# The first two token tiles loaded as rows and turned on TensorE, with the early loads on two queues paced by the warm-up matmuls

## The chip, the cores and the metric

The kernel runs on one core of a Trainium2 chip. The metric is the device time of one execution in microseconds. Where the mean granted clock of an execution was below 0.999 the text says so. "Same" means within 2% by a 95% interval. Times inside an execution count from the start of the core's span.

## The reference, cut to what matters

Two attentions over the same tokens, mixed by a gate. S is 2048 tokens, D is 1024, there are 32 heads of 32, all in bf16.

```
g = sigmoid((x * gate_w).sum(-1, keepdims=True))
a = A(x, A_wqkv, A_wo)     # linear attention, feature map elu + 1
b = B(x, B_wqkv, B_wo)     # each token attends to 8 tokens, 2 apart, backwards
out = g * a + (1 - g) * b
```

Both attentions begin with x @ wqkv. The kernel starts with the v columns of B: x (2048x1024) times 1024 columns of B_wqkv. Only the first 15 us of this product matter here.

## The kernel before

The kernel's matmuls contract over the partitions, so a tile of 128 tokens is needed turned: 128 features on the partitions, 128 tokens along the row, eight such blocks for 1024 features. The kernel lets the DMA do this (a transposing load for each of 16 token tiles, all on SyncE's queue). The weights of the first stage come in two halves of 512 columns. Each half comes in four pieces of 256 KB; a piece holds two of the eight contraction blocks.

The kernel is written as a list of operations with modelled costs and priorities; a small scheduler in the kernel's own source decides the order on every engine before the program is built. `P.op(engine, function, cost, reads, writes, prio, ...)` adds one operation.

```python
def load_x(t, prio):                        # one tile of 128 tokens, turned by the DMA
    e_, r = t // 8, t % 8
    return P.op("sp", lambda e: e.dma_start_transpose(xT[:, :, t * 128:(t + 1) * 128], x2[e_, r * 128:(r + 1) * 128, :]), 1.5, ...)

def load_w(slot, half, src, c0, prio, d0=0, d1=8, eng="sp", after=()):   # blocks d0..d1 of one half
    return P.op(eng, lambda e: e.dma_start(ws[slot][:, d0:d1, half * 512:half * 512 + 512], src[:, d0:d1, c0:c0 + 512]), ...)

load_x(0, 0)
load_w(0, 0, Bw, 2048, 0.1, 0, 2, "act")    # piece 1
load_w(0, 0, Bw, 2048, 0.2, 2, 4, "act")    # piece 2
load_w(0, 0, Bw, 2048, 0.3, 4, 6)           # piece 3
load_w(0, 0, Bw, 2048, 0.4, 6, 8)           # piece 4
for t in range(1, NT):
    load_x(t, 3 + t)
for d in range(0, 8, 2):                    # the second half, four pieces
    load_w(0, 1, Bw, 2560, 6.1 + 0.1 * d, d, d + 2)
...
for i in range(WARM):                       # WARM = 11, on a zeroed tile
    P.op("pe", lambda e: e.matmul(banks[7].ap(), warm[:, 0:128], warm[:, :], start=True, stop=True), 0.43, ...)
...
for t, half in [(4 * b + i, half) for b in range(NT // 4) for half in range(2) for i in range(4)]:
    ...
    step = 2 if t == 0 else 8               # tile 0 goes by pieces, the others in groups of 8
    for d in range(0, 8, step):
        o = group(bank, xs, w, [xr, ws[0].part((d, d + step), (half * 512, half * 512 + 512))], d, d + step)
```

So TensorE's order is: tiles 0 to 3 with the first half (32 matmuls of 128x512), tiles 0 to 3 with the second half (32 more), then tiles 4 to 7, and so on. The program fixes this order for TensorE.

## Time and profile before

| | before |
|---|---|
| median of 6 executions | 486.65 us (486.50 to 487.02) |
| TensorE busy in the profiled execution | 474.2 of 485.2 us |
| share of TensorE in the chain that ended last | 95% |
| first real matmul starts | 5.54 us |
| matmuls without a gap from | 15.30 us |

The page of the kernel before gives the busy time of each engine with its share of the span and its instruction count, and the shares of the chain that ended last:

```profile
span 485.2 us, 10105 instructions
PE 474.2 (98%) x4339; PEld 222.8 (46%) x4403; DVE 285.2 (59%) x547; ACT 140.2 (29%) x227; POOL 5.9 (1%) x36
...
PE 95%; SPq 2%; issue 1%; DMA 1%; ACT 0%; DVE 0%
```

TensorE (PE) is the bound, and its work is fixed. What is left to win is the time in which it has nothing to multiply, and that lies at the front. The timeline of TensorE shows it. Columns: start, length, engine, line, operation, out and in, shapes, number of instructions, and in brackets the idle time before with what ended it. L1373 is the warm-up, L1334 the real product.

```profile
1.25 4.01 PE L1373 MATMUL ps_all<-warm 128*128 128x512 bf16 x11 [1.25 <-DVE warm L1283]
5.54 1.47 PE L1334 MATMUL ps_all<-w,xT 128*128 128x512 bf16 x6 [0.28 <-DMA xT<-in_A_x_dram]
7.25 0.60 PE L1334 MATMUL ps_all<-w,xT 128*128 128x512 bf16 x2 [0.24 <-DMA w<-in_B_wqkv_dram]
8.17 6.82 PE L1334 MATMUL ps_all<-w,xT 128*128 128x512 bf16 x30 [0.32 <-DMA xT<-in_A_x_dram]
15.30 9.01 PE L1334 MATMUL ps_all<-w,xT 128*128 128x512 bf16 x41 [0.30 <-DMA w<-in_B_wqkv_dram]
```

Tile 0 waits for its transposing load until 5.54, then for the last weight piece until 7.25; tile 1 waits for its own load until 8.17; and the second weight half stops TensorE twice more, at 14.39 (inside the fourth line; 0.17 us over the pace) and just before 15.30. One record just before 15.30 is missing from the trace; by the spacing of the starts, 15.30 is the 40th real matmul.

A useful single number follows: matmuls of 512 columns start every 0.2158 us, so the 40th would start at 15.30 if the first had started at 15.30 - 39 x 0.2158 = 6.88 us and nothing had waited. I call this the clean start. Before: 6.88.

The issue of loads on SyncE's queue, from its timeline of the kernel before (columns as above; a DMA_TRANSPOSE is a tile of x, the others are weight pieces):

```profile
0.80 1.38 SPq L1308 DMA_TRANSPOSE xT<-in_A_x_dram  x1
2.24 1.06 SPq L1313 DMA_DIRECT2D w<-in_B_wqkv_dram  x2
3.35 4.92 SPq L1308 DMA_TRANSPOSE xT<-in_A_x_dram  x3
8.31 2.12 SPq L1313 DMA_DIRECT2D w<-in_B_wqkv_dram  x4
```

A transposing load holds the queue 1.25 to 2.27 us, a plain one about 0.5 us. The end of the windowed chain of waits of the kernel before (start, length, what) says which of these the 40th matmul hung on:

```profile
4.64 2.27 SPq L1308
...
8.31 0.58 SPq L1313
...
9.96 5.07 DMA w<-in_B_wqkv_dram
...
15.30 4.91 PE ps_all L1334 x22
```

### The profile page before, as it was taken

The page shows a single profiled execution, that of the slowest core. Times are in us where ns is not written, and L with a number is a line of the kernel's source. Part 1 is how long each engine was busy: PE and PEld are TensorE (multiplying, and loading weights), DVE is VectorE, ACT ScalarE, POOL GpSimd, SP SyncE. Part 2 cuts the span into 40 slices and gives each one's busy share as a digit, 9 for nine tenths or more (in the row PEclk, how much of TensorE's full clock was granted, in tenths as well). Part 3 has the DMA queues.
Part 4 walks back from the last instruction along what each step waited for, and adds up shares of the span by engine and source line. Part 5 has one row for each costly group of instructions (what it writes and reads, how often), then busy time and mean ns, then how long its engine had stood idle before and what let it go on. Part 6 is the DMA issues. An engine that isn't in the chain of part 4 may idle for free.

```text
span 485.2 us, 10105 instructions
## 1 busy us (share of the span) xinstructions
PE 474.2 (98%) x4339; PEld 222.8 (46%) x4403; DVE 285.2 (59%) x547; ACT 140.2 (29%) x227; POOL 5.9 (1%) x36
## 2 busy tenths in 40 slices
PE   8999999999999999999999999999999999999997
PEld 3444444444444444454544554444444444444443
DVE  2121435888688888665666556496579236653434
ACT  2111121235322234334443333455532230111000
POOL 4000000000000000000000000000000000000000
PEclk9999999999999999999999999999999999999999
DMA  8999993132014459433222322820086018830212
GB/s 224 222 194 299 309 355 122 65 110 86 1 44 135 107 138 245 100 76 86 55 75 67 85 66 66 204 54 2 10 217 163 1 15 242 221 24 2 88 68 89
DMA packets 72951, 57.39 MB, mean 118 GB/s; under 512 B 37953, under 2 KB 60865, under 8 KB 72898
## 3 DMA queue, kind: packets, MB, share of 16 engines
q1 hardware_dynamic: 72210, 56.07, 44.3%
q8 instruction: 36, 0.59, 0.5%
q10 hardware_dynamic: 688, 0.59, 0.4%
q14 instruction: 17, 0.14, 0.1%
HBM read 34.49 MB, written 13.76 MB: 99 GB/s over the span
## 4 chain that ended last, share of the span: by engine, by line
PE 95%; SPq 2%; issue 1%; DMA 1%; ACT 0%; DVE 0%
PE ps_all L1334 78%; PE ps_all L1693 11%; PE ps_all L1463 2%; PE ps_all L1440 2%; SPq L1308 1%; DMA w<-in_B_wqkv_dram 1%; PE ps_all L1556 1%; SPq L1313 1%; PE ps_all L1638 0%; PE ps_all L1610 0%; ACT e L1341 0%; DVE o L1697 0%
## 5 line engine op out<-in xcount | busy, mean ns | idle before, releaser
L1334 PE MATMUL ps_all<-w,xT 128*128 128x512 bf16 x924 | 208.6, 379 | 4.5 <-issue 2.1
L1334 PE MATMUL ps_all<-xT,w 128*128 128x512 bf16 x745 | 166.3, 379 | 2.2 <-issue 1.4
L1334 PEld LDWEIGHTS ps_all<-w,xT 128*128 128x128 bf16 x960 | 91.2, 98 | 111.1 <-DMA w<-in_B_wqkv_dram 2.1
L1334 PEld LDWEIGHTS ps_all<-xT,w 128*128 128x128 bf16 x768 | 73.9, 98 | 88.7 <-issue 1.3
L1693 PE MATMUL ps_all<-w,qT 128*128 128x512 bf16 (+1 forms) x260 | 55.4, 372 | 0.2
L1693 PEld LDWEIGHTS ps_all<-w,qT 128*128 128x128 bf16 x264 | 25.9, 98 | 29.6
L1365 DVE CAST vst<-ps_all 128x512 bf16<-128x512 f32 x15 | 10.4, 694 | 43.5 <-PE ps_all L1334 43.5
L1448 ACT ACTIVATE E<-ps_all 128x1824 bf16<-128x1824 f32 (+1 forms) x18 | 30.4, 1689 | 13.4 <-PE ps_all L1440 13.4
L1345 DVE TENSOR_SCALAR e<-e 128x512 bf16<-128x512 bf16 x64 | 18.4, 290 | 26.9 <-ACT e L1343 14.0
L1697 DVE SCALAR_TENSOR_TENSOR o<-ps_all,gm,xT 128x512 bf16<-128x512 f32 (+1 forms) x25 | 18.0, 728 | 21.1 <-PE ps_all L1693 20.8
L1341 ACT ACTIVATE e<-ps_all 128x512 bf16<-128x512 f32 x32 | 19.1, 598 | 39.0 <-PE ps_all L1334 38.1
L1343 ACT ACTIVATE e<-ps_all 128x512 bf16<-128x512 f32 x32 | 19.1, 598 | 32.3 <-PE ps_all L1334 32.3
L1295 DVE TENSOR_TENSOR mx<-mx,kT 128x1024 bf16<-128x1024 bf16 x32 | 20.9, 688 | 10.9 <-ACT kT L1366 10.8
L1295 DVE TENSOR_TENSOR mx<-mx,qT 128x1024 bf16<-128x1024 bf16 x32 | 20.8, 687 | 7.9 <-ACT qT L1369 7.9
L1451 DVE TENSOR_TENSOR E<-E,msk 128x1824 bf16<-128x1824 bf16 (+1 forms) x18 | 19.9, 1104 | 7.8 <-ACT E L1448 7.4
L1366 ACT ACTIVATE vst<-ps_all 128x512 bf16<-128x512 f32 x17 | 10.2, 601 | 48.5 <-PE ps_all L1334 45.1
L1480 DVE TENSOR_TENSOR ot<-ps_all,rs 128x512 bf16<-128x512 f32 x36 | 23.3, 686 | 0.0
L1366 ACT ACTIVATE az<-ps_all 128x512 bf16<-128x512 f32 x22 | 13.2, 601 | 34.5 <-PE ps_all L1334 34.5
L1366 ACT ACTIVATE kT<-ps_all 128x512 bf16<-128x512 f32 x20 | 11.9, 597 | 37.6 <-PE ps_all L1334 37.6
L1347 DVE SCALAR_TENSOR_TENSOR pk<-ps_all,e 128x512 bf16<-128x512 f32 x32 | 22.0, 689 | 0.7
L1369 ACT ACTIVATE qT<-ps_all 128x512 bf16<-128x512 f32 x19 | 11.4, 598 | 37.4 <-PE ps_all L1334 37.3
L1369 ACT ACTIVATE xT<-ps_all,g 128x512 bf16<-128x512 f32 x10 | 6.9, 689 | 45.1 <-PE ps_all L1334 45.1
(72 smaller groups left out, 260.2 us busy)
## 6 DMA issues: line engine op xcount, KB each, us to landing
rb<-rc_hbm SPq DMA_DIRECT2D x32, 256.0 KB, 5.2
w<-in_A_wqkv_dram SPq DMA_DIRECT2D x6, 1024.0 KB, 9.0
v<-vB_hbm SPq DMA_DIRECT2D x36, 132.0 KB, 2.7
vB_hbm<-vst SPq DMA_DIRECT2D x32, 132.0 KB, 6.2
w<-in_B_wqkv_dram SPq DMA_DIRECT2D x4, 1024.0 KB, 9.5
xn<-in_A_x_dram SPq DMA_DIRECT2D x16, 256.0 KB, 2.7
out_dram<-o SPq DMA_DIRECT2D x15, 256.0 KB, 2.1
oB_hbm<-ot SPq DMA_DIRECT2D x36, 96.0 KB, 2.2
```

The lines of the kernel that those rows point to most:

```text
L1295: P.op("dve", lambda e, m=m, op=op: e.tensor_tensor(m[:, 0:n], m[:, 0:n], src, op), 0.08 + n / 1920.0, reads=[m.all(), reg], writes=[m.all()],
L1334: last = e.matmul(bank.ap(), lhs(dc), rhs(dc), start=(dc == 0), stop=(dc == 7))
L1341: P.op("act", lambda e: e.activation(e_[:, :], bank.ap(), ACT.Exp), act(512), reads=[bank.iv], writes=[e_.all()])
L1343: P.op("act", lambda e: e.activation(e_[:, :], bank.ap(), ACT.Exp, accum_out=qe[:, col:col + 1]), act(512) + 0.1, reads=[bank.iv], writes= ...
L1345: P.op("dve", lambda e: e.tensor_scalar(e_[:, :], e_[:, :], 1.0, 1e-6, op0=ALU.min, op1=ALU.add), 0.25, reads=[e_.all()], writes=[e_.all()])
L1347: P.op("dve", lambda e: e.scalar_tensor_tensor(out=dst, in0=bank.ap(), scalar=0.0, in1=e_[:, :], op0=ALU.max, op1=ALU.add), dps(512), read ...
L1366: fa = lambda e: e.activation(dst, src(), ACT.Copy)
L1369: fa = lambda e: e.activation(dst, src(), ACT.Copy, scale=scale)
L1448: P.op("act", lambda e: e.activation(E[:, 0:32 * nq].rearrange("p (j q) -> p j q", j=4), ps[:, 4:8, 0:8 * nq], ACT.Exp), act(32 * nq), rea ...
L1451: P.op("dve", lambda e: e.tensor_tensor(ev(), ev(), m[:, :, :].rearrange("p r q -> p (r q)")[:, None, :].to_broadcast([128, 16, 2 * nq]), ...
L1480: P.op("dve", lambda e, r=r, bv=bv, h=h: e.tensor_tensor(o[:, 512 * h:512 * h + 512].rearrange("p (k i c) -> p k i c", k=2, c=32), bv()[:, ...
L1693: last = e.matmul(bank.ap(0, f1 - f0), qT[:, dc, t * 128:(t + 1) * 128], ws[3][:, dc, f0:f1], start=(dc == 0), stop=(dc == 7))
```

## The change

The intent: tiles 0 and 1 need not be turned by the slow transposing load. They are loaded plain, as rows, and TensorE turns them by multiplying with an identity (`out = rows.T @ ident`); VectorE and ScalarE copy the result out of PSUM. SyncE's queue is then free earlier for tiles 2 and 3 and for the second weight half. The first six loads are shared between SyncE's and ScalarE's queues, and the last four of them wait for a warm-up matmul each. The warm-up shrinks from 11 to 6 matmuls, since the turns go on from there. The makers of the window masks leave GpSimd's start. The core of the diff:

```diff
-    WARM = 11
+    WARM = 6
...
+        C("pool", lambda e: e.memset(ident[:, :], 0.0), 0.1, [ident.all()])
+        C("pool", lambda e: e.affine_select(out=ident[:, :], ..., compare_op=ALU.not_equal, fill=1.0, ...), 0.3, ...)
...   (the makers of the window masks move behind tile 8)
-        load_x(0, 0)
-        load_w(0, 0, Bw, 2048, 0.1, 0, 2, "act")
-        load_w(0, 0, Bw, 2048, 0.2, 2, 4, "act")
-        load_w(0, 0, Bw, 2048, 0.3, 4, 6)
-        load_w(0, 0, Bw, 2048, 0.4, 6, 8)
-        for t in range(1, NT):
-            load_x(t, 3 + t)
+        warms = [P.op("pe", <warm-up matmul>, 0.43, ...) for _ in range(WARM)]
+        def pace(o, i):
+            if i >= 0:
+                o.deps.add(warms[i])
+            ...
+        due(load_rows(0, 0, 1024, 0, "act"), 0.45, 2.7)
+        due(pace(load_w(0, 0, Bw, 2048, 0.1, 0, 2), -WARM), 0.45, 2.9)
+        due(pace(load_w(0, 0, Bw, 2048, 0.2, 2, 4), 0), 0.45, 3.7)
+        due(pace(load_rows(1, 0, 1024, 2.6, "act"), 1), 0.45, 4.5)
+        due(pace(load_w(0, 0, Bw, 2048, 2.7, 4, 6), 3), 0.45, 5.2)
+        due(pace(load_w(0, 0, Bw, 2048, 2.8, 6, 8, "act"), 4), 0.45, 6.0)
+        for t in range(2, NT):
+            o = load_x(t, 3 + t)
...
+        for t, p in [(t, p) for t in range(2) for p in range(4)]:
+            def turn(e, t=t, b=b, p=p):
+                for k in range(2):
+                    d = 2 * p + k
+                    last = e.matmul(b.ap(128 * k, 128 * k + 128), rows_[t][:, d * 128:(d + 1) * 128], ident[:, :], ...)
+                return last
+            o = P.op("pe", turn, 0.18, ...)
+            P.op("act" if p % 2 else "dve", <copy 128x256 out of PSUM into xT>, ...)
+            for i in range({3: 1}.get(4 * t + p, 0)):      # one more warm-up after the turns of tile 0
+                P.op("pe", <warm-up matmul>, 0.43, ..., after=[o])
...
-            step = 2 if t == 0 else 8
+            step = 2 if t == 0 or t == 1 and half == 0 else 8
...
+        for o in P.ops:
+            if o.eng == "sp" and o not in paced:
+                o.deps.add(warms[5])
```

`due(o, cost, at)` only tells the scheduler when to expect a load.

## The prediction

> **What bounds the kernel now.** TensorE. The page gives PE 474.2 of 485.2 us busy (98%), granted clock 1.0, and 95% of the chain that ended last. From 15.30 us on the timeline shows matmuls back to back (one start every 0.216 us); PE's later waits sum to about 3.5 us in 0.16 us pieces at mode changes, and the tail after the last matmul (482.1 to 485.2 us) is untouched. So only the front can be won.
>
> **The front before.** The windowed chain up to 15 us is SyncE issuing (transposing loads hold its queue 1.25 to 2.27 us each, plain ones about 0.5), then the last piece of the second weight half: issued 9.96, landed 15.02. The first real matmul starts at 5.54 because the first transposed tile, issued at 0.80, lands at 5.49; further waits end at 7.21 (weight piece 4), 8.13 (tile 1), 14.34 and 15.02 (second half). By 15.51 us 40 matmuls of 512 columns are out; at 0.2158 us each these need 8.63 us, so the front costs as much as a clean start at 6.88 us.
>
> **What changes.**
> - Removed: two transposing issues (1.38 and 1.25 us of SyncE), their 4.7 us landings, five warm-up matmuls. The window makers leave GpSimd's start; they were not on the chain.
> - Added: two plain 256 KB row loads (comparable ones landed in 2.5 to 2.8 us with little in flight, about 4 with four); sixteen 128-column products (estimate from the 512-column ones: 0.11 us cold, 0.055 warm each); eight 128x256 copies out of PSUM (estimate from 0.60 us on ScalarE and 0.69 on VectorE for 512 columns: about 0.4 us each), over two engines.
> - Moved: tile 2's transpose is issued at about 4.0 instead of 4.64, tile 3's at 5.3 instead of 6.95, the second weight half at 6.6 to 8.2 instead of 8.31 to 9.96.
>
> **Expected times.** Rows 0 land near 3.6, weight pieces near 3.8, 4.8, 6.1, 7.0, rows 1 near 5.5. First real matmul near 4.9; tiles 0 and 1 (16 matmuls) done near 8.0, set by the fourth weight piece; tile 2 arrives near 8.6, tile 3 near 10; 32 matmuls by 12.0, the second half landed by 13.4, 40 by 13.8 instead of 15.51. That is 1.7 us, all on the critical path, since PE is dense from there on. Most of it comes from SyncE's shorter list of issues; the bytes stay the same (12 pieces of 256 KB at 250 to 320 GB/s).
>
> **Clock.** Cold warm-ups start every 0.43 us until about 4.4, 3.2 us after the first; then 0.216. The Trainium skill, page "TensorE: Matmul & The Clock Gate", section "What's actually happening", puts the release at about 3.4 us of activity; this trace agrees. Six warm-ups end near 3.9, and the turns must bridge to there. If they leave a hole and the clock stays half for another window, up to 1.7 us of the gain is lost (8 matmuls at 0.43).
>
> **Predicted:** 485.0 us, 8 in 10 between 484.0 and 486.2. Faster by over 2%: 0.5%; within 2%: 99%; slower: 0.5%.
>
> **Right or wrong shows in:** the first real matmul (4.9 against 5.54); PE's last front wait; SyncE's issue of the second weight half (6.6 against 8.31); matmul spacing 0.216 from about 4.6 on; PE's stretch after 16 us unchanged in length.
>
> **What would make it wrong:** a late clock; the second transposing issue still held 2.3 us; DMA bandwidth, not issue, limiting the second half; a schedule that comes out different later (mode changes, bank order), worth some tenths either way.

## The result and the profile after

| | before | after |
|---|---|---|
| median of 6 executions, us | 486.65 (486.50 to 487.02) | 487.06 (486.42 to 487.51) |
| ratio of the means, 95% interval | | 1.0006 (0.9994 to 1.0019), same |
| profiled execution, us | 486.9 | 487.43 |
| clean start in the profiled execution, us | 6.88 | 7.27 |
| first matmul of the next stage, us | 62.13 | 62.53 |

A ratio here is the mean time of one kernel's fast runs over that of the other's of the same rounds, so it is not quite the ratio of the medians quoted beside it. The predicted 485.0 us and its range (484.0 to 486.2) were missed: no gain came. The median rose by 0.4 us, which is within the noise.

The page of the kernel after, the lines that answer to those shown of before:

```profile
span 485.7 us, 10140 instructions
PE 474.4 (98%) x4351; PEld 223.9 (46%) x4415; DVE 286.7 (59%) x552; ACT 140.3 (29%) x230; POOL 6.6 (1%) x38
...
PE 96%; issue 2%; DMA 1%; DVE 0%; ACT 0%; DVEq 0%
```

The bound is the same. TensorE's timeline of the kernel after, where L1312 is the warm-up, L1395 the turns (products with the identity), L1403 the extra warm-up and L1349 the real product:

```profile
1.25 2.74 PE L1312 MATMUL ps_all<-warm 128*128 128x512 bf16 x6 [1.25 <-DVE warm L1279]
4.43 1.01 PE L1395 MATMUL ps_all<-ident,rows 128*128 128x128 bf16 x8 [0.45 <-DMA rows<-in_A_x_dram]
5.24 0.63 PE L1403 MATMUL ps_all<-warm 128*128 128x512 bf16 x1
5.67 0.70 PE L1349 MATMUL ps_all<-w,xT 128*128 128x512 bf16 x2
7.21 0.59 PE L1349 MATMUL ps_all<-w,xT 128*128 128x512 bf16 x2 [0.85 <-DMA w<-in_B_wqkv_dram]
7.64 0.61 PE L1395 MATMUL ps_all<-ident,rows 128*128 128x128 bf16 x8
8.09 16.18 PE L1349 MATMUL ps_all<-w,xT 128*128 128x512 bf16 x72
```

The late waits of before (14.39 and 15.30) are gone: from 8.09 on TensorE never stops. But it begins that run with 4 matmuls done, where the kernel before had 8 done at 8.17. The first real matmul is no earlier than before (5.67 against 5.54): tile 0's rows are in at 4.30, then come eight turns at half clock, a filler and the copies out of PSUM, 1.37 us in all. Two more matmuls wait until 7.21 for weight piece 2, and the turns of tile 1 stand in line behind them.

SyncE's queue, from its timeline of the kernel after:

```profile
0.80 2.73 SPq L1309 DMA_DIRECT2D w<-in_B_wqkv_dram  x3
4.02 4.27 SPq L1304 DMA_TRANSPOSE xT<-in_A_x_dram  x2
8.34 2.13 SPq L1309 DMA_DIRECT2D w<-in_B_wqkv_dram  x4
```

The second half is issued at 8.34, not earlier than the 8.31 of before: the two transposing loads that are left hold the queue 4.27 us, 2.86 of them for tile 3's alone. Yet its last piece landed at 14.08 instead of 15.02. The windowed chain of waits of the kernel after no longer has SyncE's queue in it:

```profile
1.89 5.19 DMA w<-in_B_wqkv_dram
...
7.21 0.59 PE ps_all L1349 x2
7.81 0.45 PE ps_all L1395 x8
8.25 4.80 PE ps_all L1349 x22
```

It goes back over the turns of tile 1 to weight piece 2, which was issued at 1.89 and took 5.19 us.

Nothing changed after the front. Time of the execution minus the start of the next stage's first matmul is 424.8 to 425.1 us in every profiled execution without a gate or a hiccup (both named below), before and after alike. So the whole question is what sets the clean start.

### The profile page after: what moved, and what is told of

Read it like the earlier page. It is cut to its first block, busy times and chain, and to the rows that moved or that the text cites. A ratio compares the mean times of both kernels' runs of the same rounds, so it can differ in the third digit from the quotient of the medians.

```text
span 485.7 us, 10140 instructions
## 1 busy us (share of the span) xinstructions
PE 474.4 (98%) x4351; PEld 223.9 (46%) x4415; DVE 286.7 (59%) x552; ACT 140.3 (29%) x230; POOL 6.6 (1%) x38
## 4 chain that ended last, share of the span: by engine, by line
PE 96%; issue 2%; DMA 1%; DVE 0%; ACT 0%; DVEq 0%
PE ps_all L1349 79%; PE ps_all L1736 10%; PE ps_all L1506 2%; PE ps_all L1483 2%; DMA w<-in_B_wqkv_dram 1%; PE ps_all L1599 1%; PE ps_all L1681 0%; DVE o L1740 0%; PE ps_all L1653 0%; PE ps_all L1312 0%; ACT e L1356 0%; ACT qT L1384 0%; PE ps_all L1395 0%; DVE warm L1279 0%; DVEq L1816 0%
## 5 line engine op out<-in xcount | busy, mean ns | idle before, releaser
L1349 PE MATMUL ps_all<-w,xT 128*128 128x512 bf16 x924 | 208.5, 379 | 4.2 <-issue 2.1
L1349 PE MATMUL ps_all<-xT,w 128*128 128x512 bf16 x745 | 166.2, 379 | 2.2 <-issue 1.3
L1349 PEld LDWEIGHTS ps_all<-w,xT 128*128 128x128 bf16 x960 | 91.6, 98 | 109.8 <-issue 2.0
L1349 PEld LDWEIGHTS ps_all<-xT,w 128*128 128x128 bf16 x768 | 73.9, 98 | 88.7 <-issue 1.3
L1491 ACT ACTIVATE E<-ps_all 128x1824 bf16<-128x1824 f32 (+1 forms) x18 | 30.4, 1688 | 13.4 <-PE ps_all L1483 13.4
L1473 DVE TENSOR_SCALAR qd<-qT,par 128x912 bf16<-128x912 bf16 (+1 forms) x35 | 15.0, 452 | 9.6 <-PE ps_all L1483 9.2
```

The costliest lines, as they stand in the source:

```text
L1349: last = e.matmul(bank.ap(), lhs(dc), rhs(dc), start=(dc == 0), stop=(dc == 7))
L1491: P.op("act", lambda e: e.activation(E[:, 0:32 * nq].rearrange("p (j q) -> p j q", j=4), ps[:, 4:8, 0:8 * nq], ACT.Exp), act(32 * nq), rea ...
```

## The experiments

All landings below are read from the trace and in us. "Full clock" is the moment from which the clock records of the trace give TensorE its full clock. The page called "TensorE: Matmul & The Clock Gate" of the Trainium skill, section "What's actually happening", says that the clock is released after a busy window of about 3.4 us whose start is free-running, so that the moment varies from run to run. The section puts this variation at 500 ns either way. The records of full clock last whole multiples of 3.41 us (477.87 and 481.28 us are 140 and 141 of them), and the moment lies between 4.24 and 7.05 us in all ungated profiled executions that hold such a record, but one (e3), though the warm-up always begins at 1.25.

| run | rows 0 or tile 0 | weight pieces 1 to 4 | rows 1 or tile 1 | full clock | dense from, with so many done | next stage |
|---|---|---|---|---|---|---|
| before | 5.49 | 3.58, 5.30, 6.36, 7.21 | 8.13 | 4.24 | 8.17, 8 (two waits later) | 62.13 |
| after | 4.30 | 4.74, 7.08, 7.76, 8.51 | 6.85 | 5.87 | 8.09, 4 | 62.53 |
| after again (e1) | 4.18 | 4.69, 5.38, 6.97, 7.78 | 6.41 | 6.51 | 7.34, 4 | 61.79 |
| one queue (e2) | 3.66 | 4.45, 6.46, 7.83, 8.63 | 7.12 | 5.13 | 8.68, 6 | 62.65 |
| no pace (e3) | 4.76 | 5.24, 6.67, 8.22, 8.01 | 6.04 | 10.18 | 8.69, 4 (half clock to 9.97) | 63.82 |
| old queues (e4) | 4.38 | 4.98, 6.50, 5.78, 7.23 | 8.01 | 5.49 | 8.51, 4 | 62.90 |
| half the weights (e5) | 4.20 | 4.75, 5.09, 7.18, 7.43 | 6.61 | 4.26 | 7.23, 4 | 61.63 |
| bridge (e6) | 4.31 | 4.79, 5.89, 7.56, 7.77 | 6.17 | 5.18 | 7.61, 4 | 62.01 |
| order (e9) | 4.20 | 4.70, 5.86, 6.87, 7.61 | 6.13 | 6.42 | 7.66, 4 | 62.06 |
| bridge and order (e10) | 4.24 | 4.76, 5.42, 7.75, 8.00 | 6.67 | 6.83 | 8.04, 4 | 62.44 |
| rows first (e11) | 4.57 | 5.04, 6.47, 7.67, 8.02 | 5.73 | 4.93 | 6.83, 2 | 61.66 |
| no turn (e13) | 4.27 | 4.76, 5.44, 6.89, 7.65 | 6.13 | 7.05 | 7.24, 6 | 61.20 |

The theories to tell apart were these. The weight pieces came late because two queues share the same engines (A); because the pace held the loads back (B); or because the bytes were limited by what the DMA engines deliver at the start (D). Against all of them stands the thought (C) that TensorE's own chain, turns and copies in strict order at half clock, is what costs. Later runs add TensorE's program order (E) and the clock itself as causes. The expectations use these letters in part.

Times of all runs follow. Each is the median of the timed executions; "before" is the kernel before on the same chip in the same rounds.

| run | median, us | before, us | ratio (95%) |
|---|---|---|---|
| e1 after again | 487.05 | 486.81 | 1.0005 (0.9992 to 1.0019) |
| e2 one queue | 487.47 | 486.81 | 1.0013 (0.9999 to 1.0027) |
| e3 no pace | 487.81 | 486.81 | 1.0018 (1.0004 to 1.0032) |
| e4 old queues | 487.98 | 486.81 | 1.0029 (1.0016 to 1.0043) |
| e5 half the weights | 486.71 | 486.74 | 0.9993 (0.9980 to 1.0006) |
| e6 bridge | 486.83 | 486.74 | 1.0001 (0.9988 to 1.0014) |
| e7 second half on ScalarE | 489.73 | 486.74 | 1.0066 (1.0048 to 1.0084) |
| e8 e7 with tile 1 earlier | 489.03 | 486.74 | 1.0042 (1.0029 to 1.0055) |
| e9 order | 487.33 | 486.57 | 1.0013 (1.0000 to 1.0027) |
| e10 bridge and order | 487.28 | 486.57 | 1.0010 (0.9997 to 1.0024) |
| e11 rows first | 487.04 | 486.57 | 1.0015 (1.0001 to 1.0028) |
| e12 second half on ScalarE, mended | 486.50 | 486.57 | 1.0001 (0.9987 to 1.0014) |
| e13 no turn | 486.19 | 486.83 | 0.9998 (0.9981 to 1.0015) |
| e14 no weights | 486.76 | 486.83 | 1.0000 (0.9987 to 1.0013) |
| e15 e12 with tile 1 earlier | 487.90 | 486.83 | 1.0024 (1.0011 to 1.0037) |
| e16 before, gated | 496.14 | 486.55 | 1.0191 (1.0177 to 1.0205) |
| e17 after, gated | 496.44 | 486.55 | 1.0199 (1.0185 to 1.0213) |
| e18 no turn, gated | 495.45 | 486.55 | 1.0183 (1.0169 to 1.0197) |

e5, e13, e14 and e18 compute a wrong result; the others are correct.

### e1: the kernel after, once more

No edit.

> The changed kernel once more, to have it on the same chip as its variants. Three theories of why the gain was lost are open. A (two queues): the row loads and the weight pieces share the 16 DMA engines from two queues, the engines drift apart, and a load counts only when its slowest engine is through; so weight piece 2 and rows 1 land near 7 us together. B (pacing): the waits on warm-up matmuls make the loads start too late. C (TensorE): the warm-up gap, the cold turns and the filler matmul cost the time, whatever the loads do. All expect here again about 1.000 of before, piece 2 and rows 1 landing at 6.5 to 7.3 us and no PE wait from about 8.1 us on; a landing that moves by over 0.5 us would say that the profile of one execution is no firm ground.

The median came out at 487.05, 0.24 above before. The profiled execution was one of the quick ones (486.58). TensorE's timeline of e1:

```profile
5.55 1.50 PE L1349 MATMUL ps_all<-w,xT 128*128 128x512 bf16 x4
6.89 0.61 PE L1395 MATMUL ps_all<-ident,rows 128*128 128x128 bf16 x8
7.34 16.85 PE L1349 MATMUL ps_all<-w,xT 128*128 128x512 bf16 x75
```

Piece 2 landed at 5.38 instead of 7.08 and the dense run began 0.75 us earlier with the same 4 done: clean start 6.54 instead of 7.27. One and the same kernel thus has a front that varies by 0.7 us, and one profile of it proves nothing to a few tenths. Why piece 2 came so differently stays open.

### e2: all six loads on SyncE's queue

```diff
-        due(load_rows(0, 0, 1024, 0, "act"), 0.45, 2.7)
+        due(pace(load_rows(0, 0, 1024, 0), -1), 0.45, 2.7)
-        due(pace(load_rows(1, 0, 1024, 2.6, "act"), 1), 0.45, 4.5)
+        due(pace(load_rows(1, 0, 1024, 0.25), 1), 0.45, 4.5)
-        due(pace(load_w(0, 0, Bw, 2048, 2.8, 6, 8, "act"), 4), 0.45, 6.0)
+        due(pace(load_w(0, 0, Bw, 2048, 0.4, 6, 8), 4), 0.45, 6.0)
```

> All six early loads on SyncE's queue, in the same order and with the same pacing; the order of PE, VectorE and GpSimd is identical. A: the transfers finish one by one; from the bytes moved in the trace (3 pieces by about 4.9 us, 4 by about 5.9) piece 2 lands near 5.5 and rows 1 near 6.3, PE's long wait at 6 us shrinks from 1.0 us to under 0.3, and the kernel is 0.5 to 1 us faster than the changed kernel. B: no change, as the issue times are the same. C: no change in time even if the landings move.

487.47 against 487.05 of e1 on the same chip. Rows 0 came 0.5 us earlier (3.66), but piece 2 still at 6.46, rows 1 at 7.12 and piece 4 at 8.63. Queues are not what delays them; A falls. The skill's page "DMA: Bandwidth & Descriptors", section "Issuing engines are not separate DMA queues", says that loads issued by different engines run on the same 16 DMA engines and that several issuers save only issue time; the small difference of the medians here (0.4 us, within the intervals) does not speak against it.

### e3: no pacing

```diff
             if i >= 0:
-                o.deps.add(warms[i])
+                pass
-        due(pace(load_rows(1, 0, 1024, 2.6, "act"), 1), 0.45, 4.5)
+        due(pace(load_rows(1, 0, 1024, 2.4, "act"), 1), 0.45, 4.5)
-        due(pace(load_w(0, 0, Bw, 2048, 2.8, 6, 8, "act"), 4), 0.45, 6.0)
+        due(pace(load_w(0, 0, Bw, 2048, 2.45, 6, 8, "act"), 4), 0.45, 6.0)
```

> Two queues as in the change, but the five paced loads no longer wait for warm-up matmuls; PE order identical. B: everything lands earlier, piece 2 by 5.5 and rows 1 by 6, time 0.5 to 1 us below the changed kernel. A: more loads in flight from two queues drift at least as much: piece 2 and rows 1 land at 6.5 or later, the six together end at about the same 8.5 us, time the same within 0.3 us or worse. C: no change.

487.81, slower than e1. Without the pace rows 1 came at 6.04, but rows 0 and piece 1 came 0.6 us later (4.76, 5.24), and pieces 3 and 4 still landed at 8.0 to 8.2. The pace was not what held the last pieces back; B falls. The late rows 0 opened a hole behind the warm-up, and the clock stayed at half until 10.18. The hole may have caused the late clock, but one execution does not show it. TensorE's timeline of e3:

```profile
4.90 1.01 PE L1395 MATMUL ps_all<-ident,rows 128*128 128x128 bf16 x8 [0.91 <-DMA rows<-in_A_x_dram]
...
7.83 1.06 PE L1395 MATMUL ps_all<-ident,rows 128*128 128x128 bf16 x8
8.69 15.58 PE L1349 MATMUL ps_all<-w,xT 128*128 128x512 bf16 x67
```

Matmuls from 8.69 to 9.97 started 0.43 us apart, twice the full-clock spacing.

### e4: the loads on the queues of the kernel before, unpaced

```diff
+        due(pace(load_rows(0, 0, 1024, 0), -1), 0.45, 2.7)                  # SyncE
+        due(pace(load_w(0, 0, Bw, 2048, 0.1, 0, 2, "act"), -WARM), 0.45, 2.9)
+        due(pace(load_w(0, 0, Bw, 2048, 0.2, 2, 4, "act"), 0), 0.45, 3.7)
+        due(pace(load_rows(1, 0, 1024, 2.6), 1), 0.45, 4.5)                 # SyncE, after pieces 3 and 4
+        due(pace(load_w(0, 0, Bw, 2048, 0.3, 4, 6), 3), 0.45, 5.2)
+        due(pace(load_w(0, 0, Bw, 2048, 0.4, 6, 8), 4), 0.45, 6.0)          # pace() adds no wait here
```

> Rows and turns as in the change, but the loads issued as before it: x (now rows) 0, weight pieces 3 and 4 and rows 1 on SyncE's queue, pieces 1 and 2 on ScalarE's, none paced; PE order identical to the change's. This is the turning by TensorE alone, without the new load plan. If the transposing transfer itself was what kept the queues in step before (its marks in the trace all fall within 0.1 us), the row loads drift here too: A expects piece 2 at 6 or later. B expects piece 2 near the 5.30 it had before and a gain of about 0.7 us over the changed kernel. C expects no gain.

487.98, the slowest of the four. Piece 3 came early (5.78), and rows 1 late (8.01): TensorE stood from 6.85 to 8.05 for them. In e1 to e4 the six loads are spread differently, yet the last of them lands at 7.8 to 8.6 each time. The DMA view of the window from 2 to 8 us says why it is hard to do better; its head line for before, after and e1 in turn (packets, bytes, mean rate, packets under some sizes):

```profile
DMA packets 3812, 1.73 MB, mean 288 GB/s; under 512 B 2791, under 2 KB 3812, under 8 KB 3812
```
```profile
DMA packets 1868, 1.68 MB, mean 281 GB/s; under 512 B 597, under 2 KB 1621, under 8 KB 1868
```
```profile
DMA packets 2434, 1.82 MB, mean 303 GB/s; under 512 B 1166, under 2 KB 2190, under 8 KB 2434
```

e2 moved 1.65 MB in the same window (274 GB/s) and e3 1.71 MB (284 GB/s). Whatever the queues and the pace, 1.65 to 1.82 MB move in these 6 us. Six loads are 1.57 MB, and tiles 2 and 3 begin behind them.

### e5: half the bytes of pieces 2 to 4

```diff
-            n = d1 - d0
+            n = d1 - d0; wide = 256 if c0 == 2048 and src is Bw and d0 else 512
-            ... ws[slot][:, d0:d1, half * 512:half * 512 + 512], src[:, d0:d1, c0:c0 + 512] ...
+            ... ws[slot][:, d0:d1, half * 512:half * 512 + wide], src[:, d0:d1, c0:c0 + wide] ...
```

> Wrong on purpose: weight pieces 2 to 4 of the first half load only 256 of their 512 columns (the rest is zeroed early by GpSimd), so 0.39 MB of the first 1.57 MB is gone; every order, wait and issue is that of the changed kernel. The first runs left this theory (D, bytes): in every arrangement so far the first six loads were all in at 7.8 to 8.6 us (8.13 before the change), about 1.6 MB from 2 us on at some 270 GB/s, so the front is limited by bytes and no order or queue helps. D: piece 4 lands 0.8 to 1.3 us earlier than the 7.8 to 8.5 of the changed kernel, PE is dense from 7.0 or earlier, time 0.5 to 1 us below the changed kernel. If the number of loads and their latency set the landings, they stay and so does the time.

486.71, level with before (486.74). The last piece landed at 7.43, 0.35 to 1.2 us before the last of the six loads in after and e1 to e4. A plain bound by bytes would have taken off 384 KB, or about 1.4 us at the 281 GB/s of the kernel after (an estimate). So the bytes are at most a part of it, not the whole: D in its strong form falls.

### e6, e9, e10: no hole behind the warm-up, a fixed order on TensorE, and both

e6 adds two warm-up matmuls behind the six. e9 forces TensorE's order, so that the turns of tile 1 come before pieces 3 and 4 are waited for. e10 does both.

```diff
                  for _ in range(WARM)]
+        for _ in range(2): <warm-up matmul>                                        # e6, e10
...
+        row = [parts[k] for k in ((0, 0, 0), (0, 0, 2), (1, "turn", 0), (1, "turn", 1), (1, "turn", 2), (1, "turn", 3),
+                                  (1, 0, 0), (1, 0, 2), (0, 0, 4), (1, 0, 4), (0, 0, 6), (1, 0, 6), (2, 0, 0))]   # e9, e10
+        for a, b in zip(row, row[1:]):
+            b.deps.add(a)
```

> Two more warm-up matmuls right after the six of the changed kernel, so that PE runs without a hole from 1.25 to about 4.6 us; all else identical. In the profiles the clock turned full at about 5.8 and 6.5 us in the changed kernel and only at about 10.1 in the unpaced one, where the hole before the turns was 1.1 us. If the hole delays the clock (theory C, in part), the clock is full by 4.9 us here, the first real matmuls come every 0.216 us, and the median falls by 0.2 to 0.5 us against the changed kernel with a narrower spread. If the clock does not matter behind the load waits, the time stays within 0.2 us.

> The changed kernel with one thing altered: PE's program order in the front. In the change tile 1's matmuls stand behind all of tile 0's, so in several profiles PE stood still for weight piece 3 (in the bridged run 6.84 to 7.61 us, in the one-queue run about 1 us in three holes) while tile 1's matmuls on pieces 1 and 2 were ready. Here: tile 0 pieces 1, 2; turns of tile 1; tile 1 pieces 1, 2; then piece 3 of both, piece 4 of both. Theory E (program order) expects no PE wait over 0.3 us after the turns, and 0.2 to 0.5 us off the changed kernel's time. Theory D in its strong form (only bytes) expects no change, as the loads are the same.

> The same order plus the two bridging warm-ups. If the clock and the order each cost the change a few tenths, this is the better of both: clock full by 5.2 us, PE dense from about 7.1 with 4 of 40 matmuls done, 40th started near 14.7 (before 15.30, change 15.1 to 15.7), so 0.5 to 0.7 us below before (ratio about 0.9988).

e6: 486.83, e9: 487.33, e10: 487.28, against 486.74, 486.57 and 486.57 of before. None is a gain. In e6 the clock was full by 5.18, and TensorE then stood from 6.84 to 7.61 for piece 3. (The profiled execution of e6, 488.57, also has one hole of 1.8 us at 313.84 that nothing explains.) In e9 and e10 the turns of tile 1 come early, and the clock came late (6.42, 6.83). TensorE's timeline of e10:

```profile
4.64 1.06 PE L1396 MATMUL ps_all<-ident,rows 128*128 128x128 bf16 x8
5.49 0.63 PE L1404 MATMUL ps_all<-warm 128*128 128x512 bf16 x1
5.92 1.49 PE L1349 MATMUL ps_all<-w,xT 128*128 128x512 bf16 x4
7.24 0.61 PE L1396 MATMUL ps_all<-ident,rows 128*128 128x128 bf16 x8
8.04 16.14 PE L1349 MATMUL ps_all<-w,xT 128*128 128x512 bf16 x74 [0.18 <-DVE xT L1401]
```

From 4.64 to 8.04 TensorE is hardly ever idle, and only four real matmuls come out of it. The rest is turning, a filler that bridges the copies, and half clock. The bridge has a price too: rows 0 were in at 4.24, and the turns began at 4.64, behind the two added warm-ups; in after they began 0.13 us after the landing.

### e7, e8: the kernel before with the second weight half on ScalarE's queue

```diff
+        half2 = []
-            load_w(0, 1, Bw, 2560, 6.1 + 0.1 * d, d, d + 2)
+            half2.append(load_w(0, 1, Bw, 2560, 6.1 + 0.1 * d, d, d + 2, "act"))
+        for o in half2:
+            o.deps.add(parts[0, 0, 6])             # e8: parts[1, 0, 0]; tile 1 loaded before piece 4, tiles 0 and 1 taken by pieces
```

> On the kernel before: only the second half's weight pieces move to ScalarE's queue, issued after the first tile's matmuls, instead of waiting behind the transposing issues on SyncE. It tests the prediction's step that SyncE's list of issues delays the second half. If that is right, the two waits at 14.4 and 15.3 us (0.63 us above the pace) go and the time falls by 0.4 to 0.6 us below before; if bytes limit, the pieces or the tiles land no earlier and it stays within 0.2 us.

> On the kernel before, no rows and no turns: as the previous one, and tile 1's transposing load goes ahead of weight piece 4, with PE taking tile 0 and tile 1 piece by piece (pieces 1 to 3 of both, then piece 4 of both). With the same bytes in the same time, 12 instead of 8 matmuls are ready before the sixth load. Expected: tile 1 lands near 7.2, piece 4 near 8.1, PE dense from about 7.3 with 6 of 40 done, so 40 by 14.6 to 14.8 instead of 15.51: 0.7 to 0.9 us below before. If the landings get later with another order, less.

489.73 and 489.03: 3.0 and 2.3 us slower than before (one of e7's six executions, 491.65, had a mean granted clock of 0.997). Both were meant to win the late waits without any turning. The scheduler put SyncE's free time to use and issued tiles 4 and 5 ahead: six transposing loads in a row instead of three. The second half then arrived in company, and TensorE waited until 18.29 (e7) and 17.91 (e8). These two miss their aim because of the edit and tell nothing of the theory, except that loads let in ahead of the pieces TensorE needs next cost 2 to 3 us.

### e12: the same, with the later loads held back

```diff
+        for o in xs4:                              # tiles 4 and up
+            o.deps.add(parts[2, 0, 0])
+        row = [parts[k] for k in ((3, 0, 0), (0, 1, 0), (0, 1, 2), (0, 1, 4), (0, 1, 6), (1, 1, 0), ...)]
+        ...                                        # gate_w and the row loads wait for tile 8
```

> On the kernel before: the run with the second half on ScalarE's queue again, without its flaw (the scheduler had let two further transposing loads and their bytes go ahead of the pieces, so PE waited for those until 18.3 us). Here tiles 4 and later, the gate row and the row tiles of x wait for PE's progress, and PE keeps the order of before. If SyncE's list of issues delayed the second half: pieces land from about 11.5 to 13.7, no wait at 14.4 and 15.3, 40th start near 14.9 instead of 15.30, 0.4 us below before. If bytes or a mixed pair of queues limit: pieces land at 14 or later, no gain.

486.50, level with before's 486.57. The pieces of the second half were issued from 7.91 and the last landed at 14.14 (15.02 before); the two late waits are gone. In the profiled execution (486.38) the clean start is 6.20, in the median of the timed ones almost nothing of it is seen. It is not a version that beats the kernel before.

### e11, e15: rows 1 before piece 2; tile 1 before piece 4

e11 is the kernel after with the bridge, rows 1 unpaced ahead of piece 2, and the turns of tile 1 straight after the first two matmuls. e15 is e12 with tile 1's transposing load ahead of piece 4, and with TensorE taking tiles 0 and 1 by pieces.

```diff
-        due(pace(load_w(0, 0, Bw, 2048, 0.2, 2, 4), 0), 0.45, 3.7)                 # e11
-        due(pace(load_rows(1, 0, 1024, 2.6, "act"), 1), 0.45, 4.5)
+        due(pace(load_w(0, 0, Bw, 2048, 0.2, 2, 4), 1), 0.45, 4.5)
+        due(pace(load_rows(1, 0, 1024, 2.4, "act"), -1), 0.45, 3.7)
...
-            load_x(t, 3 + t)                                                       # e15, for tiles 1 to 3
+            load_x(t, 3 + t if t > 1 else 0.35)
```

> The bridged and reordered kernel with rows 1 loaded ahead of weight piece 2 (unpaced on ScalarE's queue), and PE taking tile 1 as soon as it is turned: with the same bytes in, two tiles times two pieces give 8 matmuls from four loads. Rows 1 expected at about 5.4, piece 2 at 6.4, 8 of 40 matmuls done by about 7.3, 40th start near 14.2; 0.9 to 1.1 us below before (ratio about 0.998). If both rows and both first pieces land together at 6.5 or later, as in the unpaced two-queue run, no better than the previous one.

> A try at a version that beats both, on the kernel before (no turns): second half on ScalarE's queue in its right order, tile 1's transposing load ahead of weight piece 4, PE taking tiles 0 and 1 piece by piece. By the fronts so far (dense start less 0.216 us for each matmul done is 6.2 to 6.5 us in the best of every arrangement) it should come out no better than the fastest ones: next stage at 61.3 to 61.7, time within 0.3 us of before. Only if tile 1 lands before 7.0 with the pieces where they were is there a gain of 0.3 to 0.6 us.

e11 gave 487.04 (before 486.57), although its profiled execution was a quick one (486.48; clean start 6.40). e15 gave 487.90: tile 1 came at 7.08, a microsecond earlier than before, and piece 4 at 8.41, a microsecond later; the last two pieces of the second half came at 14.42 and 15.32, and both late waits were back. What is brought forward pushes something else back.

### e13: the kernel of e10 without the turns

The rows are multiplied as they are, without turning, so the result is wrong. Loads, warm-up and order of the real matmuls are those of e10.

```diff
-        for t, p in [(t, p) for t in range(2) for p in range(4)]:
-            ...                                    # turns, copies and the extra warm-up are gone
+            if t < 2:
+                xs, xin = (lambda dc, t=t: rows_[t][:, dc * 128:(dc + 1) * 128]), ...
```

> Wrong on purpose: the bridged and reordered kernel without the turns; tiles 0 and 1 are multiplied as they lie in the row tiles, and their place in the turned x is filled by GpSimd. Loads, queues and pacing are those of the change. If the turning chain (landing, eight products, copies of 0.4 us, and PE's own 0.45 to 0.86 us) is what ate the gain, the first real matmul comes at about 5.0, PE is dense from 6.1 to 6.7 with 4 done, and the next stage starts near 61.2 us against 62.0 to 62.4 with turns: 0.7 to 1 us faster than the run with turns. If the loads alone set the front, under 0.3 us.

486.19 against 486.83 of before, and against e10's +0.71 over its own before on another chip: 1.35 us apart. One of its six executions took 488.62 at a mean granted clock of 0.996, where the other five had 1.000; it alone widens the interval and lifts the mean. TensorE's timeline of e13:

```profile
4.90 4.66 PE L1349 MATMUL ps_all<-w,rows 128*128 128x512 bf16 x16
9.39 3.62 PE L1349 MATMUL ps_all<-w,xT 128*128 128x512 bf16 x16
```

The first real matmul starts at 4.90, and tile 2 is reached at 9.39 instead of the 10.63 of e10. The profiled executions had almost the same moment of full clock (7.05 and 6.83) and near enough the same landings; their next stages begin at 61.20 and 62.44, or 1.24 us apart. Up to 0.27 of this may be the bridge (an estimate: the 0.40 us from landing to turn in e10, less the 0.13 of after), which e13 does not feel, since its first real matmul waits for piece 1, landed at 4.76.

### e14: the kernel of e10 without pieces 2 to 4

```diff
-        due(pace(load_w(0, 0, Bw, 2048, 0.2, 2, 4), 0), 0.45, 3.7)
-        due(pace(load_w(0, 0, Bw, 2048, 2.7, 4, 6), 3), 0.45, 5.2)
-        due(pace(load_w(0, 0, Bw, 2048, 2.8, 6, 8, "act"), 4), 0.45, 6.0)
+        <ws[0][:, 2:8, 0:512] zeroed by GpSimd>
```

> Wrong on purpose: the bridged and reordered kernel with weight pieces 2 to 4 of the first half not loaded at all but zeroed early by GpSimd; turns as in the change. 0.79 of the first 1.57 MB is gone. If the loads set the front, rows 1 lands near 5.5 and tile 2 near 7.3, PE is dense from about 5.4, and the next stage starts near 61.0 us: 1 us or more faster than the run with them. If the turning chain alone sets it, under 0.3 us.

486.76, level with before (486.83). In the profiled execution, with three quarters of the weights free of charge, rows 1 came 0.9 us earlier than in e10 (5.77), and still the dense run began at 8.05 with 4 done and the next stage at 62.45, as in e10. So weight pieces and bytes alone do not set the front of this kernel. But this execution, 487.21, was one of the two slow ones: by the medians over their own before, e14 (-0.07) lies 0.78 us below e10 (+0.71). So the weights seem to be a part of it; how large, the profile of one execution does not tell. In that execution the clock turned full at 6.87, and TensorE had been walking through cold turns, filler, cold matmuls and turns until then. Removing the wait for weights there only uncovers TensorE's chain behind it.

### e16, e17, e18: before, after and no turn, all at full clock

Here the front is played some 9 us later, after 22 further warm-up matmuls that bring the clock to full. All loads wait for a gate: two zeroings on VectorE that take the first 9.8 us. The warm-up and the pace behind the gate are set for full clock.

```diff
+        for d0, d1 in ((0, 4), (4, 7)):
+            gate = C("dve", lambda e, d0=d0, d1=d1: e.memset(qT[:, d0:d1, :], 0.0), 3.3, ...)
+        for _ in range(22):
+            C("pe", <warm-up matmul>, 0.3, ...)
+        for o in P.ops:
+            if o.chan:
+                o.deps.add(gate)
```

> The kernel before with its whole front put behind a gate: VectorE's memsets take about 7.5 us, TensorE runs 22 warm-ups meanwhile, and only then do the loads start, with 18 more warm-ups (at full clock) in place of 11. The time of the wait is the same in all three gated kernels, so they are compared with one another. Theory C (clock): the clock turns full at a random moment between about 4.4 and 8 us, so part of the front runs at half speed in some executions; with the gate every execution starts its front at full clock, and the spread of 1 us seen so far shrinks to 0.3 us or less. If the spread comes from the loads, it stays. Expected about 495 to 496 us.

> The changed kernel behind the same gate, twelve warm-ups at full clock in place of six, its paced loads on every second one, so that the issue times after the gate are those of the change. If the late clock ate the gain, this is faster than the gated kernel before by 0.7 to 1.5 us. If the loads and the turning chain ate it, the two are within 0.4 us. From the fronts: dense start of PE about 6.3 to 6.7 us after the gate with 4 done against 7.4 with 8 done and two later waits, so I expect 0.3 to 0.8 us faster.

> Wrong on purpose: the run without turns behind the same gate, so that the clock plays no part. Its distance from the gated changed kernel is what the turns cost at full clock (expected 0.5 to 0.9 us), and its distance from the gated kernel before is what the load plan alone is worth (expected 1.0 to 1.5 us faster than the gated kernel before).

| | e16 before | e17 after | e18 no turn |
|---|---|---|---|
| median, us | 496.14 | 496.44 | 495.45 |
| all, us | 495.63, 495.72, 496.14, 496.40, 496.56 | 496.09, 496.38, 496.44, 496.57, 496.61 | 495.18, 495.26, 495.45, 496.45, 496.83 |
| mean granted clock 0.997 | none | 496.44 | 495.45, 496.45, 496.83 |
| next stage, after the first issue, us | 61.36 | 61.73 | 62.18 (clock fell, see below) |

After is 0.30 us above before, as it is without the gate (0.24 and 0.41). So, as far as five executions each tell, the late or early clock is not what separates them. Nor did the spread shrink to what I had expected: e16 still spans 0.93 us, e17 0.52. Without the turns, the two executions with an undisturbed clock took 495.18 and 495.26: about 1.2 us below e17's undisturbed four (median 496.48) and 0.9 below e16.

This distance is not the price of the turns alone. e18 also fixes TensorE's order (tile 1's products on pieces 1 and 2 before piece 3), as e10 and e13 do, and e17 keeps the order of after. In e17 the copies of tile 1 were done at 16.64, yet TensorE stood 0.70 and 0.29 us for pieces 3 and 4. With the fixed order it could have been dense from about 16.25 with 4 done instead of 17.54 with 6, so up to 0.9 us of the distance may be the order (an estimate from the starts and landings of e17; tiles 2 and 3 and the second half, in at 18.30, 19.19 and 22.42, would not have stopped it). No run has the turns, the fixed order and full clock together, so whether that would beat e16 stays open. TensorE's timeline of e17 (subtract 9.79, the first issue, to compare with an ungated front):

```profile
14.48 1.09 PE L1353 MATMUL ps_all<-w,xT 128*128 128x512 bf16 x4
15.55 0.62 PE L1399 MATMUL ps_all<-ident,rows 128*128 128x128 bf16 x8
16.87 0.38 PE L1353 MATMUL ps_all<-w,xT 128*128 128x512 bf16 x1 [0.70 <-DMA w<-in_B_wqkv_dram]
17.54 6.65 PE L1353 MATMUL ps_all<-w,xT 128*128 128x512 bf16 x30 [0.29 <-DMA w<-in_B_wqkv_dram]
```

At full clock the front of the kernel after waits for weight pieces 3 and 4 instead: it is dense from 7.76 after the first issue (17.54 less 9.785) with 6 done. The front of e16 was dense from 17.50 - 9.79 = 7.71 with 8 done, and waits once more near 14 us:

```profile
15.33 1.93 PE L1338 MATMUL ps_all<-w,xT 128*128 128x512 bf16 x8 [1.45 <-DMA xT<-in_A_x_dram]
17.50 6.65 PE L1338 MATMUL ps_all<-w,xT 128*128 128x512 bf16 x29 [0.24 <-DMA xT<-in_A_x_dram]
```

In the profiled execution of e18 the clock fell back. Its windows of 2 us (PE busy, PEld busy, VectorE, ScalarE, GpSimd, then granted clock, share of DMA, GB/s):

```profile
12.00:14.00 2.00, 0.58 (x3) 0.08 (x1) 0.00 (x0) 0.00 (x0) 0.00 (x0) 1.00 0.88 257
14.00:16.00 2.00, 1.33 (x5) 0.34 (x6) 0.00 (x0) 0.00 (x0) 0.00 (x0) 1.00 1.04 350
16.00:18.00 2.00, 2.00 (x6) 0.71 (x5) 0.00 (x0) 0.00 (x0) 0.00 (x0) 0.54 1.26 270
18.00:20.00 2.00, 2.00 (x6) 0.76 (x6) 0.00 (x0) 0.07 (x1) 0.00 (x0) 0.61 1.02 285
20.00:22.00 2.00, 1.95 (x10) 0.93 (x10) 0.69 (x1) 0.53 (x1) 0.00 (x0) 1.00 0.89 288
```

TensorE stood 1.89 us for the first weight piece, up to 14.47, and from 16.16 to 19.57, 3.41 us, it ran at half clock. The executions at a mean clock of 0.997 are most likely the same event, e13's 488.62 too; for them only the mean was recorded.

## Why the prediction was wrong, point by point

- **That TensorE is the bound and only the front can be won: right.** After the front, 424.8 to 425.1 us follow in every case.
- **"First real matmul near 4.9": wrong, 5.67 (e1: 5.55).** Nearly all of the miss is the landing of the rows, 4.30 instead of 3.6. Behind it the prediction allowed 1.3 us, and 1.37 were measured: eight products at half clock (0.81 us from the first to the filler's start), a filler, copies of 0.4 us each on two engines. Without the turns the first real matmul did start at 4.90 (e13).
- **"Rows 1 5.5, weight pieces 3.8, 4.8, 6.1, 7.0": wrong.** They landed at 6.85 and at 4.74, 7.08, 7.76, 8.51. The prediction took the landing times of loads in light traffic (2.5 to 2.8 us, about 4 with four in flight); here all six were in flight from 3.60 to 4.30, 256 KB took up to 5.2 us from issue to landing, and six loads were never all in before 7.6 us in any arrangement that carried their full bytes.
- **"Tiles 0 and 1 (16 matmuls) done near 8.0, set by the fourth weight piece": this is the step that failed.** At 8.09 four were done, in e1 four at 7.34, and the 17th matmul, the first of tile 2, started at 10.73 (e1: 9.99). The prediction had the chain turn, copy, product of tile 0 on the path, and nearly right. But it let weight piece 4 alone set the end of tiles 0 and 1, and so took the rest of TensorE's chain, above all the turns of tile 1 that stand in line between real matmuls, to be hidden behind that wait. It was not: with turns, copies and filler taken out and the rest kept, tile 2 is reached at 9.39 instead of 10.63 (e13 against e10). This is 1.24 us between profiled executions and 1.35 by the medians over their own before, up to 0.27 of it the bridge. The rest of the delay, 9.39 against 8.0, comes with later landings (piece 4 at 7.65 in e13, not 7.0) and a later clock; how it splits between them stays open.
- **The load plan: right in its direction, too large in size.** Where tiles 0 and 1 come as rows and nothing is turned, e13 gains 0.64 us on before by the medians and e18 gains 0.69 on e16 (0.9 with an undisturbed clock), instead of the 1.7 predicted; both also have the fixed order. The gain of e13 less the chain is e10's loss of 0.71 by construction, so the sum is no check of its own; the kernel after itself lost 0.41 and 0.24, and 0.30 behind the gate. The sizes are medians of five or six executions that spread over up to a microsecond, and the intervals of the means overlap, so they hold to some 0.3 us.
- **"Most of it comes from SyncE's shorter list of issues", second half issued at 6.6: wrong, 8.34 (7.60 in e1).** The prediction's own warning came true: the second transposing load, issued at 5.43 and allowed 1.3 us, held the queue 2.86 us (2.12 in e1). The second half was in at 14.08 all the same, 0.94 earlier than before, and the two late waits (0.43 us over the pace) fell away. But TensorE now came to it later: its 40th matmul started at 15.69, not 15.30. The gain on the loads was turned into slack.
- **"The second half landed by 13.4; 40 by 13.8": wrong, 14.08 and 15.91** (e1: 13.68 and 15.18; the 40th matmul is out 0.22 us after its start). In clean starts: 5.17 was predicted, 7.27 and 6.54 were measured.
- **The clock: a spread, and not shown to be the cause.** It turned full at 5.87 and 6.51 instead of the 4.4 the prediction took for granted, but also at 4.26 to 7.05 in other kernels, and with the clock out of the way before and after stay 0.30 apart (e16, e17). In e3 a hole of 1.1 us went with a clock that was late by a window, as the prediction feared; in one execution, so that it is not shown to be the cause.

Two things are shown: that the turning chain lies on the critical path while the clock comes late (e13 against e10), and that the whole difference lies in the front. What the chain costs at full clock is not shown, since e18 changes the order too. That the front is several nearly equal limits (TensorE's chain, the loads, the clock), each uncovering the next when it is removed, is what e5, e6, e9, e10 and e14 suggest together: each alone removes one, and none of them beats before, though e14 is faster than e10 by the medians. How much each is worth by itself stays open. So does what lets piece 2 land at 5.38 in one execution and at 7.08 in another. No version tried beats both kernels; the fastest with a correct result, e12, is level with before.

## What to carry to other kernels

Before moving work from a DMA to TensorE at the start of a kernel, write down the new chain with every step in it (landing, product at half clock, copy out of PSUM, next product, in TensorE's strict order), for every tile and not only the first, and set it beside the arrival of the other loads; in e10 and e13 about 1.2 us of chain ate a gain of about 0.7. A load that lands earlier is worth only what TensorE would have waited for it, so ask first when TensorE gets there under the new plan. And look at a front in several executions before believing one: the same kernel had two fronts 0.7 us apart.

## What the Trainium skill lacked or had wrong

- "TensorE: Matmul & The Clock Gate", the table in "Why this matters for your kernels", warns of idle gaps over about 3 us between bursts. In e18 a gap of 1.89 us was followed by 3.41 us at half clock from 16.16 on; in the 3.41 us before that TensorE was busy 1.49 us. In e3 a hole of 1.1 us between warm-up and turns was followed by a full clock only at 10.18 us, and after holes of 0.5 to 0.7 us (after, e1, e4, e5, e9) it came by 6.51. The page has no bound for gaps shorter than a window.
- The same page, section "What's actually happening", gives 500 ns either way for the moment of full clock. Here it lay between 4.93 and 7.05 us in the five kernels with the bridge (e6, e10, e11, e13, e14), whose TensorE is busy alike from 1.25 to 4.6 us.
- The same page, section "Wait — 56ns, not 53.3ns?", gives start-to-start times of 106.7 and 426.7 ns cold and 55.6 and 215.7 ns warm for 128 and 512 columns. The trace agrees (107, 427, 55 and 216 ns); nothing to mend.
- The same page, section "Part 4: PE-mode transpose", says that the output goes to PSUM and needs a copy after. It lacks what the chain costs a front: 1.24 to 1.35 us here for two tiles with a late clock (e13 against e10, up to 0.27 of it the bridge), done with plain products against an identity.
- "DMA: Bandwidth & Descriptors" has no figure on this chip for how long the issue of a transposing load of a 128x1024 tile holds the queue: 1.23 to 3.11 us in the first 20 us here, against about 0.5 us for a plain load of 256 KB.
- I found no page that says what a handful of loads costs at the start of a kernel: 256 KB took up to 5.2 us from issue to landing in the kernel after and 6.4 us without the pace (e3), 274 to 309 GB/s moved between 2 and 8 us in every ungated run that carried the full bytes, and the same load of the same kernel landed 1.7 us apart in two executions.
